# Matmuls on zeros in TensorE's opening gaps, one store for an output tile, and the last tile in reused memory

## Chip, cores and metric

One core of one Trainium2 chip. The time is the device time in microseconds (us) of one execution; lower is better. Fast executions of one kernel here spread over about 1.5% (354 to 359 us for the kernel before). PE is TensorE, DVE VectorE, ACT ScalarE, POOL GpSimd, SP SyncE, whose only work here is to issue transfers. "Clock" is the TensorE clock that was granted, as a share of full speed. A DMA transfer is moved in packets by up to 16 DMA engines; the profile shows packets and their sizes, not which engine moved them.

## The reference

Attention with RMS-normalised queries and keys (batch 8, 12 heads, 448 rows, head dimension 64), then a feed-forward stage with two multiplied branches:

```python
q_n, k_n = rmsnorm(q, g_q), rmsnorm(k, g_k)
attn = softmax(q_n @ k_n.T / sqrt(64))
x = (attn @ v) moved to (3584, 768)      # rows (b, s), columns (h, d)
h = (x @ w1) * (x @ w2) @ w3             # d_ff = 1024
out = h @ w_out                          # (3584, 768), float32
```

## The kernel before

A planner runs while the program is built: it simulates all engines with fixed durations and fixes the order of every instruction on every engine. Work for ACT, DVE, SP and POOL is added as jobs with an engine, an assumed duration, a key and what it needs; `pe_step` chooses what PE does next. `w3 @ w_out` is multiplied once, so that an output tile is one product of `abT` with `w34s`.

The columns of `abT` are ordered (j, p) within a batch, where output row = 7 p + j, p is 0 to 63 and j 0 to 6. A tile of 128 columns is thus two values of j with 64 rows each, in partitions 0 to 63 and 64 to 127. Each half is stored by its own transfer:

```python
            def store(x):
                nc.sync.dma_start(
                    out=out_rows(bp, t, x),          # [64, 768]: 64 rows, 7 rows apart
                    in_=hold["o"][HP * x : HP * x + HP].rearrange("p z n -> p (z n)"),
                )
            ...
                for x in range(2):
                    add("SP", 0.57, -20.0, lambda x=x: store(x), ...)
...
    def pe_step(t):
        took = pe_try(t, t - MARGIN)
        return pe_try(t, t) if took is None else took
...
    def do_last(t, z):                               # the last tile, in two halves
        ...
        o_sb = out_pool.tile([128, 2, NH], FP, tag="o_sb", name="o_sb")
...
        nc.vector.memset(warm_t, 0.0)
        ...
        warm(WARM)                                   # 15 matmuls of 512 columns on zeros
```

(The lines with "..." leave parts out, and the comments are added here.)

## Time and profile before

| | before |
|---|---|
| median of 3 runs | 357.58 us (355.82 to 359.0) |
| span of the profiled run | 355.0 us, clock 0.995 |
| PE busy | 97% |
| stores of the output | 54 of 192 KB, 4 of 96 KB |

The prediction below shows PE's side of this profile. What turned out to matter lies with the transfers. From the page: what was moved in how many packets; for the two large queues (q1 is SP's, q0 GpSimd's) packets, MB and the share of the 16 DMA engines' time; and the stores (count, KB each, median us from issue to landing).

```profile
DMA packets 68360, 55.11 MB, mean 155 GB/s; under 512 B 44932, under 2 KB 62244, under 8 KB 68292
...
q1 hardware_dynamic: 49824, 36.51, 43.2%
q0 software_dynamic: 18016, 16.92, 27.5%
...
out_dram<-o_sb SPq DMA_DIRECT2D x54, 192.0 KB, 3.4
```

With the three small queues the shares sum to 72.5%: packets under way for 257 of 355 us per DMA engine, on the average of the 16. (Packets can overlap: in several stretches below the share is above 1. So 257 us is an upper figure for how long an engine was occupied.) SP's queue where the first output tiles leave (start, duration, line, what, count):

```profile
86.73 2.80 SPq L953 DMA_DIRECT2D out_dram<-o_sb  x4
90.17 3.32 SPq L516 DMA_TRANSPOSE qkT<-qks  x2
93.58 0.54 SPq L344 DMA_DIRECT2D qk_sb<-in_q_dram  x1
```

Four stores are followed at once by two transposes of queries and keys, 1.7 us each, on which the next scores depend, and by the next loads. All stand in one queue.

### The profile page before, as it was taken

The numbers are of one execution on the slowest core, as the hardware profiler recorded it, in microseconds if no ns is written. First come the engines' busy times: TensorE is split into PE (matmuls) and PEld (weight loads), VectorE is DVE, ScalarE is ACT, GpSimd is POOL, SyncE is SP. The second block draws the span as 40 slices with busy tenths as digits, with TensorE's granted clock in tenths as the row PEclk, the third lists the DMA queues.
The fourth block names the chain that finished last, engine by engine and source line by source line (L and its number), as shares of the span: only waits on it lengthen the run. The fifth ranks groups of instructions, "written<-read, shape, count | busy, mean of one in ns | idle before, by whom it ended". The sixth has DMA issues, their size and how long they took to land.

```text
span 355.0 us, 16130 instructions
## 1 busy us (share of the span) xinstructions
PE 344.0 (97%) x7352; PEld 224.0 (63%) x7352; DVE 213.2 (60%) x300; ACT 256.0 (72%) x368; POOL 75.3 (21%) x132
## 2 busy tenths in 40 slices
PE   6899999999999999999999999999999999999994
PEld 2577666656665667656657675677665656666673
DVE  4459476997998689898659757686633321222100
ACT  4579958988979999898889898766886942222122
POOL 7266633105200504013013050320320000000000
PEclk9899999999999999999999999999999999999999
DMA  8999999579997899995988959942690014000064
GB/s 191 243 262 166 254 297 253 129 159 194 237 210 201 160 173 248 228 264 56 215 241 114 244 82 259 227 52 42 119 176 2 4 46 110 29 4 2 4 179 136
DMA packets 68360, 55.11 MB, mean 155 GB/s; under 512 B 44932, under 2 KB 62244, under 8 KB 68292
## 3 DMA queue, kind: packets, MB, share of 16 engines
q1 hardware_dynamic: 49824, 36.51, 43.2%
q0 software_dynamic: 18016, 16.92, 27.5%
q8 instruction: 57, 0.93, 1.1%
q10 hardware_dynamic: 452, 0.66, 0.6%
q14 instruction: 11, 0.09, 0.1%
HBM read 46.66 MB, written 11.01 MB: 162 GB/s over the span
## 4 chain that ended last, share of the span: by engine, by line
PE 84%; DMA 6%; ACT 5%; DVE 1%; POOL 1%; issue 1%; SPq 0%; DVEq 0%; POOLq 0%; ACTq 0%
PE ps_all L817 61%; PE ps_all L716 11%; PE ps_all L631 9%; DMA qk_sb<-in_q_dram 5%; PE ps_all L695 2%; ACT w_outs L653 1%; ACT P L653 1%; ACT sq L419 1%; PE ps_all L1064 1%; DMA out_dram<-o_sb 1%; ACT a_sb L329 1%; POOL w3s L397 0%; DVE qks L449 0%; PE ps_all L1086 0%; POOL w_outs L403 0%
## 5 line engine op out<-in xcount | busy, mean ns | idle before, releaser
L653 ACT ACTIVATE P<-ps_all 128x896 bf16<-128x896 f32 x120 | 104.5, 923 | 17.6 <-PE ps_all L631 17.3
L368 POOL DMA_DIRECT2D v_sb<-in_v_dram x96 | 57.2, 616 | 173.6 <-PE ps_all L631 75.4
L817 PE MATMUL ps_all<-xT,w1s 64*64 64x448 bf16 x1536 | 88.7, 349 | 0.0
L817 PE MATMUL ps_all<-xT,w2s 64*64 64x448 bf16 x1536 | 88.6, 349 | 0.0
L817 PE MATMUL ps_all<-w34s,abT 64*64 64x384 bf16 x1728 | 80.7, 323 | 0.0
L897 DVE TENSOR_TENSOR abT<-ps_all,a_sb 128x896 bf16<-128x896 f32 x32 | 34.9, 1089 | 50.8 <-PE ps_all L817 50.6
L817 PEld LDWEIGHTS <-abT 64*64 64x64 bf16 x1728 | 52.2, 107 | 19.5 <-issue 0.6
L631 PE MATMUL ps_all<-qkT 64*64 64x448 bf16 x672 | 62.0, 357 | 1.6 <-ACT w_outs L653 0.8
L817 PEld LDWEIGHTS <-w1s 64*64 64x64 bf16 x1536 | 48.7, 107 | 23.4 <-issue 0.4
L817 PEld LDWEIGHTS <-w2s 64*64 64x64 bf16 x1536 | 48.1, 107 | 24.1 <-issue 0.5
L426 DVE TENSOR_REDUCE ssq<-sq 128x14 f32<-128x896 f32 (+1 forms) x50 | 51.3, 1041 | 13.7 <-ACT sq L419 13.3
L449 DVE TENSOR_TENSOR qks<-qk_sb,al 128x448 bf16<-128x448 f32 x96 | 55.7, 617 | 1.8 <-ACT al L438 1.7
L419 ACT ACTIVATE sq<-qk_sb 128x896 f32<-128x896 f32 (+1 forms) x50 | 45.1, 916 | 4.0 <-DMA qk_sb<-in_q_dram 3.6
L329 ACT ACTIVATE a_sb<-ps_all 128x896 bf16<-128x896 f32 x22 | 20.2, 919 | 29.7 <-PE ps_all L817 29.7
L758 DVE TENSOR_TENSOR xT<-ps_all,r 128x448 bf16<-128x448 f32 x48 | 27.4, 616 | 13.1 <-ACT r L739 10.8
L335 DVE COPY o_sb<-ps_all 128x768 f32<-128x768 f32 (+1 forms) x16 | 14.1, 881 | 32.9 <-PE ps_all L1006 15.8
L631 PEld LDWEIGHTS <-qkT 64*64 64x64 bf16 x672 | 22.7, 107 | 15.3 <-issue 6.1
L329 ACT ACTIVATE o_sb<-ps_all 128x768 f32<-128x768 f32 (+1 forms) x15 | 11.2, 746 | 23.7 <-PE ps_all L817 22.0
L716 PE MATMUL ps_all<-P,v_sb 128*32 128x448 bf16 x480 | 26.7, 352 | 0.0
L817 PE MATMUL ps_all<-w_outs,w3T 64*64 64x384 bf16 x512 | 25.0, 324 | 0.5 <-DVE w3T L335 0.4
L716 PEld LDWEIGHTS <-v_sb 128*32 128x32 bf16 x608 | 16.6, 97 | 12.0
L653 ACT ACTIVATE w_outs<-ps_all 128x896 bf16<-128x896 f32 x24 | 21.2, 915 | 3.5 <-PE ps_all L631 3.2
(60 smaller groups left out, 225.5 us busy)
## 6 DMA issues: line engine op xcount, KB each, us to landing
out_dram<-o_sb SPq DMA_DIRECT2D x54, 192.0 KB, 3.4
qk_sb<-in_q_dram SPq DMA_DIRECT2D x18, 448.0 KB, 4.3
qk_sb<-in_k_dram SPq DMA_DIRECT2D x18, 448.0 KB, 5.2
v_sb<-in_v_dram POOLq DMA_DIRECT2D x48, 64.0 KB, 3.9
v_sb<-in_v_dram POOLq DMA_DIRECT2D x48, 48.0 KB, 4.1
qk_sb<-in_q_dram POOLq DMA_DIRECT2D x5, 448.0 KB, 10.5
qk_sb<-in_k_dram POOLq DMA_DIRECT2D x5, 448.0 KB, 10.9
w3s<-in_moe_w_dram POOLq DMA_DIRECT2D x8, 256.0 KB, 8.2
```

The costliest lines, as they stand in the source:

```text
L329: nc.scalar.activation(out=out, in_=in_, func=AF.Copy, scale=1.0 if by is None else by)
L335: nc.vector.tensor_copy(out=out, in_=in_)
L368: nc.gpsimd.dma_start(out=v_bufs[i % 4][p0 : p0 + HP, g::2, 0 : j1 - j0].rearrange("p h j d -> p h (j d)"), in_=src[:, g::2, j0:j1].rearra ...
L419: nc.scalar.activation(out=s["sq", t][:, x0:x1], in_=src[:, t, x0:x1], func=AF.Square)
L426: nc.vector.tensor_reduce(out=s["ssq"][:, t, x0:x1], in_=s["sq", t][:, x0:x1], axis=AX, op=ADD)
L449: nc.vector.tensor_tensor(out=s["qks"][:, t, :, x], in0=src[:, t, x], in1=s["alpha"][:, t, x].unsqueeze(2).broadcast_to([NP, NJ, D]), op=MULT,
L631: nc.tensor.matmul(out=sc[HP * c : HP * c + HP, u, 0:S].rearrange("p (j s) -> p j s", j=NJ), lhsT=qkT[u * D : (u + 1) * D, 1, j, cols], rh ...
L653: lambda: nc.scalar.activation(out=dst, in_=sc[:, :, 0:S], func=AF.Exp),
L716: nc.tensor.matmul(out=ps_all[hd * HALF : (hd + 1) * HALF, z, 0:S], lhsT=value_weights(i, hd, j, kind), rhs=s["P"][:, hd, j, :] if j < NF ...
L758: lambda: nc.vector.tensor_tensor(out=xT[b][:, 2 * m + kind - 1, :], in0=ps, in1=s["r"], op=MULT),
L817: mm = nc.tensor.matmul(out=ps_all[64 * h : 64 * h + 64, p.bank + z, 0 : p.n], lhsT=lhsT[64 * r : 64 * r + 64, 64 * h : 64 * h + 64], rhs= ...
L897: nc.vector.tensor_tensor(out=abT[bp][:, f0 : f0 + 2, odd * S : (odd + 1) * S], in0=ps_all[:, z : z + 2, 0:S], in1=a_sb[b, f0], op=MULT,)
```

## The change

Three parts: keep PE's clock up while it waits for the first data; store 18 of the 28 output tiles by one instruction in place of two; spare the last copies a wait for a buffer.

```diff
@@ ffn2_pair: one store for a tile that lies in one batch
+            flat = lambda: hold["o"].rearrange("p z n -> p (z n)")
+            whole = bp < B // 2 - 1 and 2 * t // NJ == (2 * t + 1) // NJ
...
+            def store_whole():
+                bb, j = divmod(2 * t, NJ)
+                r0 = (2 * bp + bb) * S
+                rows = out[r0 : r0 + S].rearrange("(p j) n -> j p n", j=NJ)
+                nc.sync.dma_start(out=rows[j : j + 2], in_=flat())
...
+                if whole:
+                    add("SP", 0.6, -20.0, store_whole, ..., moves=(1.1, 0.14))
+                    return
@@ do_last
-        o_sb = out_pool.tile([128, 2, NH], FP, tag="o_sb", name="o_sb")
+        spare = qk_bufs[0].rearrange("p w x j d -> p (w x j d)")
+        o_sb = spare[:, x * NH : (x + 1) * NH].rearrange("p (z n) -> p z n", z=1)
@@ pe_step (WARM_TO = 13.0, WARM_N = 256)
-        return pe_try(t, t) if took is None else took
+        took = pe_try(t, t) if took is None else took
+        if took is None and t < WARM_TO and idle_banks(t):
+            return do_warm(single(idle_banks(t)))       # one matmul on zeros
+        return took
```

The output side of `store_whole` has the shape [2, 64, 768]: two values of j outermost, then 64 rows, then 768 columns.

More of the change, by code (lines that the diff above doesn't have):

```diff
@@ L243 @@
     WARM = 15
+    WARM_TO = 13.0
+    WARM_N = 256
     MAX_PAIRS = 2
@@ L950, in copy @@
                 copy_on(engine, hold["o"], ps_all[:, z : z + 2, 0:NH])
+            flat = lambda: hold["o"].rearrange("p z n -> p (z n)")
+            whole = bp < B // 2 - 1 and 2 * t // NJ == (2 * t + 1) // NJ
             def store(x):
                 nc.sync.dma_start(
-                    out=out_rows(bp, t, x),
-                    in_=hold["o"][HP * x : HP * x + HP].rearrange("p z n -> p (z n)"),
-                )
+                    out=out_rows(bp, t, x), in_=flat()[HP * x : HP * x + HP]
+                )
+            def store_whole():
[3 more added lines that the diff above has]
+                nc.sync.dma_start(out=rows[j : j + 2], in_=flat())
             def copied(e):
                 freed(z)(e)
+                if whole:
+                    add(
+                        "SP", 0.6, -20.0, store_whole,
+                        needs=[lambda: e + SEM], moves=(1.1, 0.14),
+                    )
+                    return
                 for x in range(2):
@@ L1126, in pe_step, with do_warm @@
         took = pe_try(t, t - MARGIN)
-        return pe_try(t, t) if took is None else took
+        took = pe_try(t, t) if took is None else took
+        if took is None and t < WARM_TO and idle_banks(t):
+            return do_warm(single(idle_banks(t)))
+        return took
+    def do_warm(z):
+        nc.tensor.matmul(
+            out=ps_all[:, z, 0:WARM_N], lhsT=warm_t[:, 0:128], rhs=warm_t[:, 0:WARM_N],
+            start=True, stop=True,
+        )
+        into("t")
+        return pass_us(WARM_N)
     def start_pv(t, size, idle):
```

## The prediction

> **What bounds the kernel now.** I read the page first, then PE's waits, then the clock and busy time stretch by stretch, then the instructions of the opening and of the end in order of time. The page's busy shares and slices:
>
> ```profile
> PE 344.0 (97%) x7352; PEld 224.0 (63%) x7352; DVE 213.2 (60%) x300; ACT 256.0 (72%) x368; POOL 75.3 (21%) x132
> ...
> PE   6899999999999999999999999999999999999994
> ...
> PEclk9899999999999999999999999999999999999999
> ```
>
> PE is busy almost everywhere and no other engine is near it, so PE is the bound. The one slice in which the clock falls below 9 tenths is the second, from 8.9 to 17.8 us. PE's waits:
>
> ```profile
> PE ps_all L1064 <- DVE qks L449: 2.3, 2, 1.8
> PE ps_all L1244 <- DVE warm_t L1227: 1.2, 1, 1.2
> PE ps_all L631 <- ACT w_outs L653: 0.8, 2, 0.4
> PE ps_all L631 <- DVE qkT L335: 0.7, 1, 0.7
> ```
>
> All named waits of PE sum to about 7 us, most of it before 12 us. A check that busy is also fed: four 64x64 quarters run together, and the chain shows ten such groups of 448 columns in 1.89 us, 0.189 us a group. The FFN's first stage has 3072 matmuls, 768 groups, 145 us; the 384-column products 2240 matmuls, 560 groups at 0.163, 91 us; scores 168 groups, 32; probabilities times values 228 groups, 43; half-row sums about 7; transposes and the last tile about 10. That is 328 us of the 341.5 between the first transpose (8.8 us) and the last matmul (350.3). Only some 13 us are slack, scattered. Now the opening, by stretches. Columns: stretch, its length, then busy time with counts of PE, PEld, DVE, ACT, POOL, then the clock, the DMA share and GB/s:
>
> ```profile
> 7.00:10.50 3.50, 1.14 (x15) 0.79 (x14) 3.43 (x9) 0.52 (x2) 0.58 (x1) 1.00 1.15 207
> 10.50:11.20 0.70, 0.02 (x4) 0.02 (x4) 0.62 (x1) 0.00 (x0) 0.41 (x1) 0.81 1.07 199
> 11.20:12.00 0.80, 0.80 (x8) 0.17 (x8) 0.00 (x0) 0.18 (x1) 0.19 (x1) 0.50 1.13 213
> 12.00:13.00 1.00, 1.00 (x12) 0.77 (x8) 0.00 (x0) 1.00 (x2) 0.59 (x1) 0.50 1.14 209
> 13.00:14.00 1.00, 1.00 (x10) 0.26 (x10) 0.69 (x1) 0.86 (x2) 0.59 (x1) 0.50 1.14 206
> 14.00:14.70 0.70, 0.70 (x12) 0.59 (x16) 0.00 (x0) 0.70 (x2) 0.17 (x1) 0.76 1.16 211
> ```
>
> PE does 1.16 us of work between 7.0 and 11.2, and then its clock stands at half from about 11.0 to 14.4: a stretch of about 3.4 us, exactly when the first scores and the first w3 transposes come. The same work cold and, later, warm:
>
> ```profile
> 11.18 0.96 PE L631 MATMUL ps_all<-qkT 64*64 64x448 bf16 x8 [0.72 <-DVE qkT L335]
> 12.07 1.03 PE L1086 MATMUL ps_all<-ident,w3s 128*128 128x128 bf16 x8
> 13.04 0.96 PE L631 MATMUL ps_all<-qkT 64*64 64x448 bf16 x8
> 13.93 0.80 PE L1086 MATMUL ps_all<-ident,w3s 128*128 128x128 bf16 x8
> ...
> 15.44 0.62 PE L1086 MATMUL ps_all<-ident,w3s 128*128 128x128 bf16 x8
> ...
> 36.40 0.57 PE L631 MATMUL ps_all<-qkT 64*64 64x448 bf16 x8
> ```
>
> The end, in order of time:
>
> ```profile
> 347.48 2.83 PE L1006 MATMUL ps_all<-w34s,abT 128*64 128x192 bf16 x64
> ...
> 350.54 0.33 ACT L329 ACTIVATE o_sb<-ps_all 128x192 f32<-128x192 f32 x1 [1.13 <-DMA out_dram<-o_sb]
> 350.71 0.36 DVE L335 COPY o_sb<-ps_all 128x192 f32<-128x192 f32 x1 [1.35 <-DMA out_dram<-o_sb]
> ```
>
> The last two copies wait for an earlier store out of the same buffer, but PE had only just finished, at 350.31.
>
> **What the skill says.** The Trainium skill, "TensorE: Matmul & The Clock Gate", Part 1 (HAM clock gate), states that PE runs at 1.2 GHz after an idle window of about 3.4 us and at 2.4 GHz after a busy one, the window running free of the kernel. The trace agrees: 0.50 for about 3.4 us, after 4.2 nearly empty microseconds. The same page, "Back-to-back issue gap", gives N/2.4 ns + 2.5 warm; 448 columns make 0.189 us, which is what the chain measures, so one filling matmul of 256 columns is estimated at 0.109 us. "DMA: Bandwidth & Descriptors", "Anatomy of one DMA", puts some 2 us of fixed time, mostly completion, on each transfer; here a 96 KB store at the end landed in 2.7 us. "Perfetto Trace Analysis" warns in its opening note that matmul busy time is a bad measure since matmuls are pipelined; hence my count by groups, which gives 328 us where the page says 344.
>
> **The change part by part.**
>
> *Filling.* The build's planner emits one 256-column matmul on zeros wherever PE would have nothing to do before its time 13.0. Idle places from 7.0 to 13: about 1.8 us before the first transpose, 0.5 before the second, 0.7 before the first scores, a few tenths after: near 4 us, so some 35 matmuls of 0.109 us. They lie in time that PE does not use; a mistimed one delays real work by about a tenth. What they buy is the cold stretch: scores 2 x (0.96 - 0.57) = 0.78 us, transposes (1.03 - 0.62) + (0.80 - 0.62) = 0.59, the first w34 products 0.84 against about 0.67 = 0.17: 1.5 us of PE time. Not all of it can be taken. POOL's waits show the first three pieces of w3 landing at about 12.0, 13.3 and 14.5. With a warm clock the second transposes could begin at 13.35 rather than 13.93, four groups of products would follow until 14.6, the third transposes would end at 15.1 rather than 15.99: **about 0.85 us** gained at that point. From 15.4 to 24.2 PE works without a gap, its 144 matmuls from 18.2 at 0.168 us a group, so the gain passes through; after that PE is full until 110 us. I take 0.7 us at the end, the rest lost to data that lands no sooner (the DMA share is near full up to 53 us).
>
> *One store per tile.* 28 tiles, less the last, make 54 stores of 192 KB; six tiles of seven in the first three pairs of batches lie in one batch, so 36 stores become 18 of 384 KB. The bytes and rows are the same. It removes 18 issues of 0.57 us from SP, 10 us of a queue that nothing waits for long, and 18 completions that no copy waits for: apart from the last two, no o_sb copy is shown waiting for a store. The last pair of batches keeps its split stores. **0 us**, give or take the order that the planner makes of it.
>
> *The last tile.* Its copies go to memory that was the first queries', long dead. The first half waited for PE alone and took 0.1 us to start (matmuls half done at 348.9, copy at 349.00). The second half could start at 350.42 instead of 350.54 and 350.71; the later one counts, as both stores wait for both halves: **0.3 us**.
>
> Sum: 0.7 + 0 + 0.3 = 1.0 us. From the median of 357.58 that is 356.6. The three runs before spread over 3.2 us; if part of that is where the cold window falls, filling removes bad cases, and I put the expected time a little lower, at **356.2**.
>
> **The rivals.** (1) *The gain dies in the opening.* q, k and w3 arrive as before; PE waits in a new place for w3, the second half of w_out (landing about 18.3) or the first weights at 51 us. For it: the DMA share above 1 from 3.5 to 29 us. Against: w3's fourth and fifth pieces have landed by about 24.6 but are used at 26.96, and after 29 us PE shows no wait for a DMA. Time then 357.2. (2) *Fillers get in the way.* If the planner thinks a result comes later than it does, or if zeros run at half clock for the first microseconds, real work queues behind them. The first transposes came at 8.83; 13 fillers cold would end at about 9.8. Against: the clock was 1.00 from 7.0 to 10.5. Time then up to 358.5. (3) *The new order matters more than the parts.* The planner fixes the order of all engines at the build, and small shifts early, or fewer stores, change who goes first between 60 and 150 us, where ACT is also 85 to 99% busy and PE loses 0.85 us between 110 and 120. Nothing in the profile tells the sign; I allow 2 us either way. (4) *Every microsecond counts in full*: 1.5 and a little from the stores give 355.3.
>
> **Range and chances.** A 2% change is 7.15 us. All that the profile offers to these three parts is 1.8 us; only a lucky or unlucky order could add more, and the slack of PE altogether is 13 us. So within 2% is nearly certain: 0.95, faster 0.03, slower 0.02. The range is the 1 us gain with 2 us for order and about 1 us for run to run, combined: 353.8 to 358.4.
>
> **What would show it.** The clock should read 1.00 in all stretches from 7 to 18 us, eight scores take 0.57 us and eight transposes 0.62, and the products after the third transposes begin 0.6 to 1.0 us earlier. Some 30 to 40 new matmuls of about 0.11 us spacing should stand between 7 and 13. The stores should number 36 + 4, and no stretch after 60 us change by more than its order explains. The last two copies should start within 0.15 us of PE's end. The prediction is wrong if the order after 60 us moves PE's gaps by more than 2 us, if PE stays cold despite fillers, or if fillers delay the first transposes beyond 9.1.

## The result, and the profile after

| | before | after |
|---|---|---|
| median | 357.32 us (4 runs) | 439.31 us (437.34 to 440.02, 4 runs) |
| ratio of fast runs | | 1.228 (1.2215 to 1.2353) |
| profiled span, clock | 355.0 us, 0.995 | 437.1 us, 0.932 |

A ratio is the mean time of one kernel's fast runs over that of the other's fast runs of the same rounds, so not quite the ratio of the medians. The change costs 23%; within 2% had been given 0.95.

Of the page after, the lines that answer to those above and to those in the prediction:

```profile
PE 367.9 (84%) x7380; PEld 240.9 (55%) x7380; DVE 213.2 (49%) x299; ACT 258.2 (59%) x369; POOL 75.4 (17%) x132
...
PE   8999999990699967799778797724998689999996
...
PEclk9999999996879978989989999876999699999999
DMA  9999995995986999996979979954239910111036
...
DMA packets 67819, 55.10 MB, mean 126 GB/s; under 512 B 44392, under 2 KB 61704, under 8 KB 67752
...
q1 hardware_dynamic: 49284, 36.51, 55.7%
...
out_dram<-o_sb SPq DMA_DIRECT2D x18, 384.0 KB
out_dram<-o_sb SPq DMA_DIRECT2D x18, 192.0 KB
```

PE has 28 matmuls more (7380 against 7352), the fillers. Its first slice is up from 6 to 8 tenths, and the first nine slices show no loss. From the tenth slice, about 98 us, PE has holes, and in them the clock falls. PE is also busy 23.9 us longer (367.9 against 344.0 us), of which the fillers are about 3. SP's queue moved the same 36.51 MB, but its packets took 55.7% of 437 us in place of 43.2% of 355. The page counts 541 fewer packets, 540 of them from the class under 512 bytes.

The stretch from 90 to 130 us, before and then after (columns as in the prediction):

```profile
90.00:130.00 40.00, 39.15 (x864) 25.07 (x860) 32.36 (x46) 37.34 (x54) 7.13 (x12) 1.00 0.94 198
```

```profile
90.00:130.00 40.00, 24.55 (x456) 14.43 (x452) 17.84 (x24) 18.67 (x26) 2.38 (x4) 0.79 1.08 138
```

The compute engines do between a third and two thirds of the work that they did before. The DMA engines count as no less busy (1.08 against 0.94) but move 138 GB/s in place of 198. What PE waits for is in SP's queue and in PE's instructions after the first new stores:

```profile
85.24 2.20 SPq L966 DMA_DIRECT2D out_dram<-o_sb  x2
88.68 16.00 SPq L518 DMA_TRANSPOSE qkT<-qks  x2
104.78 0.61 SPq L346 DMA_DIRECT2D qk_sb<-in_q_dram  x1
...
108.86 0.59 PE L633 MATMUL ps_all<-qkT 64*64 64x448 bf16 x4 [10.50 <-DMA qkT<-qks]
```

The two transposes that took 3.32 us take 16.00, the next loads are issued at 104.8 in place of 93.6 us, and PE stands 10.5 us for the transposed queries and keys. PE's holes go on to about 380 us; the last whole-tile store is issued at 382.7, and the stores of the last batches are still in halves.

The trace's DMA records tell how the store travels. Its 3072-byte packets (one row each) were counted by how many were under way at the same time:

```
us with n store packets under way      n = 1    2    3   4-12  13 and more
before                                    9.5  2.0  1.7   14.9   28.2
after                                    11.1  135.2 6.2   3.6   11.9
```

After, 135 us pass with exactly two packets under way, at a median 0.121 us for 3072 bytes, 25 GB/s each; before, half of the time 13 or more. That is what a store moved by **two DMA engines** looks like. The page's packet count says the same: if each engine that takes part writes one small completion packet, 36 stores over 16 engines wrote 576, and 18 over two write 36. The difference is 540, the number found.

The reason can be looked up. The Trainium skill, "DMA: Bandwidth & Descriptors", section "Why a DMA increments its semaphore by 16 and not by 1", paragraph on the number of engines: the largest number up to 16 is taken that divides the size of the slowest dimension on both sides. For [64, 768] that is 16; for [2, 64, 768] it is 2. The trace agrees, with its 540 packets and 135 us.

### The profile page after: what moved, and what is told of

The parts are those of the page before. It is cut to its first block, busy times and chain, and to the rows that moved or that the text cites. A ratio compares the mean times of both kernels' runs of the same rounds, so it can differ in the third digit from the quotient of the medians.

```text
span 437.1 us, 16154 instructions
## 1 busy us (share of the span) xinstructions
PE 367.9 (84%) x7380; PEld 240.9 (55%) x7380; DVE 213.2 (49%) x299; ACT 258.2 (59%) x369; POOL 75.4 (17%) x132
## 2 busy tenths in 40 slices
DMA packets 67819, 55.10 MB, mean 126 GB/s; under 512 B 44392, under 2 KB 61704, under 8 KB 67752
## 3 DMA queue, kind: packets, MB, share of 16 engines
q1 hardware_dynamic: 49284, 36.51, 55.7%
q0 software_dynamic: 18016, 16.92, 23.9%
## 4 chain that ended last, share of the span: by engine, by line
PE 64%; DMA 13%; ACT 10%; issue 5%; SPq 4%; DVE 3%; DVEq 0%; ACTq 0%
PE ps_all L819 46%; PE ps_all L718 7%; PE ps_all L633 6%; DMA qk_sb<-in_q_dram 6%; DMA qk_sb<-in_k_dram 5%; ACT P L655 4%; SPq L518 3%; ACT sq L421 2%; DMA qkT<-qks 2%; PE ps_all L1273 1%; ACT w_outs L655 1%; PE ps_all L697 1%; DVE qks L451 1%; ACT r L740 1%; PE ps_all L1081 1%
## 5 line engine op out<-in xcount | busy, mean ns | idle before, releaser
L819 PE MATMUL ps_all<-xT,w2s 64*64 64x448 bf16 x1536 | 97.8, 368 | 16.1 <-issue 13.1
L819 PE MATMUL ps_all<-xT,w1s 64*64 64x448 bf16 x1536 | 97.6, 366 | 6.8 <-issue 6.8
L633 PE MATMUL ps_all<-qkT 64*64 64x448 bf16 x672 | 68.4, 367 | 29.4 <-DMA qkT<-qks 14.8
L819 PEld LDWEIGHTS <-w2s 64*64 64x64 bf16 x1536 | 54.0, 112 | 42.1 <-issue 19.4
L819 PEld LDWEIGHTS <-w1s 64*64 64x64 bf16 x1536 | 55.0, 112 | 31.2 <-issue 10.0
L819 PEld LDWEIGHTS <-abT 64*64 64x64 bf16 x1728 | 56.1, 107 | 19.1 <-issue 3.7
L451 DVE TENSOR_TENSOR qks<-qk_sb,al 128x448 bf16<-128x448 f32 x96 | 55.7, 617 | 3.8 <-ACT al L440 3.7
L633 PEld LDWEIGHTS <-qkT 64*64 64x64 bf16 x672 | 27.4, 109 | 46.5 <-issue 22.5
L718 PE MATMUL ps_all<-P,v_sb 128*32 128x448 bf16 x480 | 29.9, 373 | 9.2 <-issue 9.2
L655 ACT ACTIVATE Pr<-ps_all 128x896 bf16<-128x896 f32 x24 | 22.3, 929 | 3.4 <-PE ps_all L633 3.4
L331 ACT ACTIVATE o_sb<-ps_all 128x768 f32<-128x768 f32 x13 | 10.5, 810 | 22.0 <-PE ps_all L819 22.0
```

The source lines that it names most:

```text
L331: nc.scalar.activation(out=out, in_=in_, func=AF.Copy, scale=1.0 if by is None else by)
L451: nc.vector.tensor_tensor(out=s["qks"][:, t, :, x], in0=src[:, t, x], in1=s["alpha"][:, t, x].unsqueeze(2).broadcast_to([NP, NJ, D]), op=MULT,
L633: nc.tensor.matmul(out=sc[HP * c : HP * c + HP, u, 0:S].rearrange("p (j s) -> p j s", j=NJ), lhsT=qkT[u * D : (u + 1) * D, 1, j, cols], rh ...
L655: lambda: nc.scalar.activation(out=dst, in_=sc[:, :, 0:S], func=AF.Exp),
L718: nc.tensor.matmul(out=ps_all[hd * HALF : (hd + 1) * HALF, z, 0:S], lhsT=value_weights(i, hd, j, kind), rhs=s["P"][:, hd, j, :] if j < NF ...
L819: mm = nc.tensor.matmul(out=ps_all[64 * h : 64 * h + 64, p.bank + z, 0 : p.n], lhsT=lhsT[64 * r : 64 * r + 64, 64 * h : 64 * h + 64], rhs= ...
```

## The experiments

Theory A: the two engines are the whole loss. Rivals: B, the planner's new order of all engines; C, a new wait on the reused memory; D, a single large transfer with one completion; E, the number or size of transfers. All results were correct. "Before" was run beside each group.

### One part at a time

The kernel before with each part alone, and the change without its store.

**Filling alone**

> The kernel before with the filling matmuls alone. Theory A (the single store of a whole tile, moved by two of the 16 DMA engines, is the whole loss): 355.5 to 356.5 us, about 1.4 us faster than before, clock 1.00 from 7 to 18 us, first output copy near 84.3 us as in the changed kernel. Rival B (the filling reshuffles the order of all engines so badly that loads and transposes come late): over 400 us.

**Whole-tile store alone**

> The kernel before with only the store of a whole tile by one transfer. Theory A: 435 to 445 us, with stretches of 70 to 100 GB/s and transposes that take 8 to 16 us to issue after each such store; 540 small packets fewer than before (36 x 16 completion writes become 18 x 2). Rival B: within 1% of 357.

**Last tile alone**

> The kernel before with only the last tile's copies put into the first queries' memory. Theory A: 0.2 to 0.3 us faster, so 357.0 and not separable from before by time; in the trace the last two copies start within 0.15 us of PE's end. Rival C (the reused memory brings a new wait): slower, with a wait on a load or a scaling of the first queries before the last copies.

**Filling and last tile**

> The changed kernel without the whole-tile store: both other parts. Theory A: 355 to 356.5 us, which is what the prediction said for all three parts. Rival B: over 400 us.

| | median, runs | ratio to before |
|---|---|---|
| before | 356.61 (39) | |
| filling | 357.58 (12) | 1.0003 (0.9978 to 1.0028) |
| whole-tile store | 434.01 (4) | 1.215 (1.206 to 1.224) |
| last tile | 355.81 (12) | 0.9993 (0.9964 to 1.0022) |
| filling and last tile | 356.76 (20) | 1.0016 (0.9995 to 1.0037) |

The store alone makes 77 of the 82 us; the other 5 come only with the other parts added and are not explained. Neither of the other parts loses time without it, so rivals B (for the filling) and C fall. The median of 434 is a little under the expected 435, and its page has the expected 44392 small packets. (Its profile is of a slow run; nothing else is read from it.) Filling does not gain the expected 1.4 us: that was a miss, taken up below. Of the last tile, the trace shows what time cannot. Second half of the last tile, with the change of memory alone:

```profile
346.12 2.83 PE L1006 MATMUL ps_all<-w34s,abT 128*64 128x192 bf16 x64
...
348.98 0.36 DVE L335 COPY qk_sb<-ps_all 128x192 f32<-128x192 f32 x1 [0.96 <-PE ps_all L1006]
348.99 0.33 ACT L329 ACTIVATE qk_sb<-ps_all 128x192 f32<-128x192 f32 x1 [0.99 <-PE ps_all L1006]
```

The copies start 0.03 and 0.04 us after PE's end at 348.95; before it was 0.23 and 0.40. The estimated 0.3 us is there (0.40 to 0.04 for the later copy, one profile each), below what 12 runs resolve.

### The same order, the same bytes, other engines

```diff
@@ f1: the changed kernel, every order kept, two transfers for a tile
-                nc.sync.dma_start(out=rows[j : j + 2], in_=flat())
+                for x in range(2):
+                    nc.sync.dma_start(
+                        out=rows[j + x], in_=flat()[HP * x : HP * x + HP])
@@ f2: one transfer, outermost dimension 64
+                nc.sync.dma_start(
+                    out=rows[j : j + 2].rearrange("x p n -> p x n"), in_=flat())
@@ f2: for that, the products are written with the two j interleaved by column
+   out=abT[...].rearrange("k (t p x) -> k t x p", x=2), in0 and in1 as "k (t x p) -> k t x p"
@@ f3 (n = 62), f4 (n = 48), d1 (n = 49), d2 (n = 57): the kernel before, each half store cut
+                for p0, p1 in ((0, n), (n, HP)):
+                    nc.sync.dma_start(out=out_rows(bp, t, x)[p0:p1], in_=...[p0:p1])
```

> The changed kernel with its own order of every engine (the planner still sees one store of 0.6 us per whole tile), but each of the 18 whole-tile stores written as two transfers of 64 rows. Theory A (two engines of 16): 355 to 357 us. Rival B (the order that the planner made of fewer stores): stays at 435 to 440 us.

> The changed kernel, 18 stores of 384 KB by one transfer each, but with the two rows of a pair in neighbouring partitions, so that the output side's outermost dimension is 64 and not 2. VectorE writes the products in that order, in three instructions instead of one, which the planner does not know. Theory A: 355 to 360 us (the extra instructions may cost 1 to 3 us). Rival D (a single transfer of 384 KB with one completion is what blocks the queue, however many engines move it): 430 us or more. Small packets: 540 minus 18 x 14 = 288 fewer than before if 16 engines take part.

> The kernel before, no other part of the change, with every 64-row store cut into 62 and 2 rows, each of which 16 does not divide: two engines each. Same order of engines, less per transfer than before. Theory A: 190 KB over two engines at about 25 GB/s each is 3.7 us, half as long as a whole tile but twice as many, so a loss of the same kind, 390 to 450 us. Rivals B and D: within 2% of the control with 48 and 16 rows.

> The control for the run with 62 and 2 rows: the same number of transfers and bytes, cut into 48 and 16 rows, both multiples of 16. Theory A: 357 to 360 us, no more than the additional 54 issues cost. Rival E (more or smaller transfers are what hurts): as slow as 62 and 2.

| | stores | engines each | median, runs | ratio |
|---|---|---|---|---|
| before | 54 of 192 KB | 16 | 356.62 (54) | |
| changed | 18 of 384 KB, 18 of 192 KB | 2 and 16 | 439.31 | 1.228 |
| f1 | 54 of 192 KB | 16 | 357.61 (20) | 1.0034 (1.0010 to 1.0058) |
| f2 | 18 of 384 KB, 18 of 192 KB | 16 | 358.78 (20) | 1.0064 (1.0042 to 1.0086) |
| f3 | 54 of 186 KB, 54 of 6 KB | 2 and 2 | 497.57 (4) | 1.394 (1.386 to 1.401) |
| f4 | 54 of 144 KB, 54 of 48 KB | 16 and 16 | 359.93 (19) | 1.0087 (1.0054 to 1.0121) |

The engines of each row follow from the rule and are confirmed by the small packets. The page lines of f2, f3 and f4 in that order:

```profile
DMA packets 68072, 55.11 MB, mean 155 GB/s; under 512 B 44644, under 2 KB 61956, under 8 KB 68004
```

```profile
DMA packets 67712, 55.11 MB, mean 111 GB/s; under 512 B 44284, under 2 KB 61596, under 8 KB 67644
```

```profile
DMA packets 69224, 55.11 MB, mean 152 GB/s; under 512 B 45796, under 2 KB 63108, under 8 KB 69156
```

Against the 44932 of before: f2 has 288 fewer (18 stores fewer, 16 packets each); f3 648 fewer (54 x 4 in place of 54 x 16); f4 864 more (54 x 32 in place of 54 x 16). All fit exactly. (f4's page is of a slow run; only counts are read from it.)

f1 has, instruction for instruction, the changed kernel's order on PE, DVE, ACT and POOL, and comes back to 357.6: rival B falls entirely. Its SP queue at the place of the 16 us:

```profile
85.30 4.31 SPq L967 DMA_DIRECT2D out_dram<-o_sb  x4
89.71 2.63 SPq L518 DMA_TRANSPOSE qkT<-qks  x2
92.43 0.55 SPq L346 DMA_DIRECT2D qk_sb<-in_q_dram  x1
```

f2 has the single 384 KB transfers and loses nothing but 0.6%: rival D falls. (Part of that 0.6% may be the extra VectorE instructions, three where there was one; this was not separated.) f3 and f4 carry no part of the change and issue equally many transfers; only the place of the cut differs, and it makes 138 us: rival E falls. f3's loss was larger than the expected range of 390 to 450. That expectation reckoned with twice as many slow stores as in the change; 54 against 18 is three times as many.

### How the loss grows, and whether another queue helps

> The kernel before with its 64-row stores cut into 49 and 15 rows: 7 and 15 engines if the number is the largest up to 16 that divides the rows. 54 x 150 KB over 7 engines at 25.4 GB/s is 0.85 us each, a quarter of the 3.75 us of 62 rows over two. Theory A with a dose: 360 to 372 us, between the 360 of 48 and 16 rows and the 498 of 62 and 2. A rival in which any number that 16 does not divide is handled slowly: near 498. Small packets: 54 x 22 - 864 = 324 more than before.

> The kernel before with its 64-row stores cut into 57 and 7 rows: 3 and 7 engines. Estimate by load per engine: the page of before has 72% of the span on each engine, 257 us; 54 x 57 packets of 0.121 us on three engines are 124 us each in place of an even share of 26, so 355 us of work on the busiest three. The same sum gives 377 for the changed kernel, which took 60 us more than that, and 437 for 62 and 2 rows, which also took 60 more. Theory of the overfull engine: 385 to 425 us, about 415. Rival (the loss grows with the bytes times the time of one store alone): 54 x 2.3 us x 0.65 = 80, so 437. Small packets: 54 x 10 - 864 = 324 fewer than before.

> The changed kernel with its whole-tile stores, still 2 x 64 rows and so still two engines, issued by ScalarE's queue instead of SyncE's, where all q and k loads and the transposes are issued. Theory F (loads and transposes stand behind the store in the same queue on those two engines): most of the loss goes, under 375 us, and no transpose takes 8 us to issue. Rival G (two engines are simply overfull, whichever queue feeds them): 420 us or more.

> The changed kernel with its whole-tile stores, 2 x 64 rows, issued by GpSimd. If GpSimd's transfers choose engines by the same rule, two of 16: 420 us or more. If they use all 16: 357 to 362 us, and the store's packets run about 12 at a time as in before.

| | engines | estimated work of the busiest engine | median, runs |
|---|---|---|---|
| before | 16 | 257 us | 357 |
| d1, rows 49 and 15 | 7 and 15 | about 281 us | 363.5 (2, one of them slow; fast 360.5) |
| d2, rows 57 and 7 | 3 and 7 | 359 us | 427.6 (2) |
| changed | 2 and 16 | 377 us | 439.3 (4) |
| f3, rows 62 and 2 | 2 and 2 | 437 us | 497.6 (4) |
| h1, changed, store from ACT's queue | 2 | | 431.0 (2) |
| h2, changed, store from GpSimd's queue | 2 to 4 by its packets | | 434.0 (4, one slow) |

By the small packets the rule holds for d1 and d2 too: 45256 and 44608 are 324 more and 324 fewer than before, as expected.

The estimate: 257 us for every engine from the page of before, less an even share of the store's packets at their median of before, 0.134 us, plus those packets at 0.121 us each on the engines that carry them (the smaller pieces on the same ones; the 355 in d2's expectation leaves them out). For the changed kernel: 18 x 128 packets are 279 us, 139 on each of two engines, in place of 19, so 257 + 139 - 19 = 377. While the sum stays well below the kernel's time the loss is small (d1); where it reaches the time, it is large. Where the loss is large, the measured times lie 61 to 69 us above the estimate; that this is the opening without stores and the waits in between is argued, not shown. d2 came out at 427.6, above the expected 385 to 425 and between the 415 that this sum gave beforehand and the 437 of its rival: it does not decide between the two. That the loss grows as the engines become fewer is shown.

Another queue does not help. From ACT's queue (h1) the time is 431 and two transposes at 102 us still take 13.75 us, so it is not a matter of standing behind the store in SP's queue alone:

```profile
102.06 13.75 SPq L518 DMA_TRANSPOSE qkT<-qks  x2
```

From GpSimd's (h2) the small completion packets are 16 per store (4451 of them in all, where the changed kernel has 4199 and before 4739), but the data still went in the main two, and at times four, packets at once (68 and 26 us), at 434 us. The access pattern is at fault, not the issuer.

h2 also speaks against reading the estimate as the cause. A store that travels alone there has two packets under way, and with four each packet still takes the same 0.234 us for its 6144 bytes; so two stores were then moved at once, most likely by different engines, and the work does not all lie on the same two. Yet the loss is nearly as large. That a store occupies its two engines for about 8 us (64 packets of 0.121 us each), and that transfers which need a share of them wait that long, would fit h2 as well as the other runs; neither this nor that one engine's total runs over is shown.

### What the filling does

The window in which the first scores run, in filling alone, and in the kernel with the last tile alone, which has no fillers but happened to keep its clock:

```profile
11.20:14.70 3.50, 3.50 (x57) 2.10 (x56) 1.38 (x2) 3.05 (x4) 1.76 (x3) 1.00 1.14 208
```

```profile
11.20:14.70 3.50, 3.50 (x60) 2.07 (x56) 1.38 (x2) 3.27 (x4) 1.75 (x3) 1.00 1.13 208
```

Both have 1.00 where the first profile of before had 0.50 to 0.76. So the cold stretch need not be there without fillers. The fast runs of before, sorted by the clock of the whole run, on the three chips of the first 12 runs: clock 0.999 or more, mean 355.6 us (25 runs); 0.993 to 0.996, like the first profile (0.995, with one stretch of 3.4 us at half clock), 356.2 us (28 runs); under 0.990, mean 358.1 us (38 runs). One cold stretch thus goes with 0.6 us. The runs under 0.990 take 2.5 us more and must have been at half clock for over 7 us (1% of 355 us, twice). Where, is not shown, since no such run of before was profiled; f4's profile (0.991, a slow run without fillers) has 0.50 from 10.3 to 17.1 us. But the filled kernels with 0.999 or more take 357.0 us (filling alone, 8 runs; filling and last tile, 12 runs), 1.4 us more than before takes when it is warm. Three runs look for the reason.

```diff
@@ g1: fillers by hand, unknown to the planner, in a fixed bank: 13, 7 and 8
+            fill(13)                      # after the opening's last warm(1)
+        if i == 0:
+            fill(8 if w else 7)           # after the two first transposes
@@ g2: g1 and the last tile's memory         @@ g3: only the 8
```

> The kernel before with the same 28 filling matmuls (13, 7 and 8) written in at the three places by hand, so that the planner does not know of them and every other instruction keeps the order of before. In the runs so far before takes about 355.5 us where its clock was full and 358 where it fell, while the planned filling takes 357.1 with a full clock. Theory P (the few instructions that the planner moved cost what the filling gains): full clock in every run and 355 to 356 us, about 1 us faster than before. Rival Q (the fillers themselves, or loads that come no sooner, cost it): 356.8 to 357.5 us.

> The same with the last tile's copies in the first queries' memory: the two harmless parts in the order of before, the version that should be best if Theory P holds. Theory P: 354.7 to 355.8 us. Rival Q: about 357.

> The order of before with only the 8 filling matmuls ahead of the first scores. If 8 keep the clock full in nearly every run and it is the fillers' number that costs the filled kernels 1.4 us against before's full-clock runs: 355.5 to 356. If loads that land no sooner take the lead back whatever fills the gap: 356.8 to 357.3 with a full clock. If 8 do not keep it warm: as before, 356.7 with clocks spread from 0.988 to 1.

| | median, runs | ratio | clocks |
|---|---|---|---|
| g1 | 356.99 (22) | 1.0013 (0.9994 to 1.0032) | 0.993 to 1.000 |
| g2 | 357.22 (22) | 1.0010 (0.9986 to 1.0034) | 0.993 to 1.000 |
| g3 | 355.88 (6) | 0.9969 (0.9930 to 1.0008) | 0.994 to 1.000 |

g1 keeps the order of every instruction of before (its trace agrees) and shows the same as the planned filling: theory P falls, it is not the few moved instructions. Where the lead goes is seen from the start of the softmax sums (the first matmuls on P and ones of a pair of head groups) in one profile each, in us:

| | at 3rd mark | 7th | 11th | 12th | 14th |
|---|---|---|---|---|---|
| before (cold) | 46.05 | 128.66 | 220.72 | 247.57 | 286.39 |
| last tile alone (warm by chance) | 44.67 | 126.88 | 219.12 | 246.21 | 285.03 |
| filling alone | 45.03 | 127.18 | 220.13 | 247.99 | 286.80 |
| g1 | 45.21 | 127.42 | 218.95 | 248.13 | 286.94 |
| g3 | 44.70 | 126.92 | 218.41 | 245.47 | 284.28 |

All warm openings lead by 0.8 to 1.4 us at 45 us and by 1.2 to 1.8 at 127. g1 gives its lead back between the 11th and the 12th mark, at one pair of loads. Last tile alone, then g1: the issue of the load, and the squares that wait for it:

```profile
213.36 1.59 SPq L344 DMA_DIRECT2D qk_sb<-in_q_dram  x1
...
219.28 2.04 ACT L419 ACTIVATE sq<-qk_sb 128x896 f32<-128x896 f32 x2 [0.95 <-DMA qk_sb<-in_q_dram]
```

```profile
213.41 0.96 SPq L344 DMA_DIRECT2D qk_sb<-in_q_dram  x1
...
221.64 2.04 ACT L419 ACTIVATE sq<-qk_sb 128x896 f32<-128x896 f32 x2 [3.47 <-DMA qk_sb<-in_q_dram]
```

The load is issued at the same time, but its data are used 8.2 us after and not 5.9. g2 shows the same place (7.9 us); filling alone has lost most of its lead before the 11th mark, between 127 and 151 us, and some there. Why the load takes longer in the filled kernels is open: nothing in the traces ties it to 28 fillers at 7 to 11 us. With 8 fillers the lead stays, and the mean of six runs is 0.3% below before, but the interval reaches 1: a hint that fewer fillers suffice, not a finding. No version here is shown to beat before; g3 is the best candidate.

## Why the prediction was wrong

**The bound.** PE was the bound, rightly read, with a slack of some 13 us. But "no other engine is near it" was said of the compute engines, and the DMA engines, with their 72%, were not weighed. (Two slips on which nothing large rests: PE's named waits sum to 5.9 us, not about 7; and the idle places listed for the fillers sum to 3 us and some tenths, not near 4.)

**The store** is the step that failed: "The bytes and rows are the same. It removes 18 issues of 0.57 us from SP, 10 us of a queue that nothing waits for long ... **0 us**". Bytes and rows are the same, but not the access pattern, and with it the number of DMA engines fell from 16 to 2. The term put at 0 us measured +77 us alone (434.0 against 356.6), of +82 in the change (439.3 against 357.3). That "nothing waits for long" for SP's queue held of before only: with two engines carrying 139 us of store packets each in place of 19, two transposes behind the first such stores took 16.0 us in place of 3.3, and PE stood 10.5 us for them. The rule was to be had beforehand, on the page of the Trainium skill named above; it was not held against the new shape. None of the four rivals had it: where they speak of stores, they look for the effect in order and time saved.

**The filling.** The mechanism was right as far as 127 us: the clock is 1.00, the first eight scores take 0.57 us, and a lead of 1.2 us stands at the third transposes (14.26 in place of 15.44) and of 1.2 to 1.8 at 127, more than the 0.85 estimated for 16 us. One term of it did not exist: the first w34 products took 0.84 us warm as cold. The fillers were 28 where some 35 were guessed, and the first transposes, at 8.6 us, were not delayed. Of the 0.7 us at the end nothing is seen: filling alone changed the time by 0.1 us (-0.8 to +1.0), which does not exclude a gain of 0.7; filling and last tile by 0.6 (-0.2 to +1.3), which does. In the profiles the lead is given back at loads past 127 us; that is the prediction's first rival, but far later than it was placed. The guess that the spread of before is partly the cold stretch fits: runs with a full clock took 355.6, with one stretch's worth of low clock 356.2, with more 358.1 us.

**The last tile.** About 0.36 us by the trace, 0.3 as worked out, and too little to be seen in the times.

**The range.** "All that the profile offers to these three parts is 1.8 us" is a bound on gains. It was used as a bound on losses too, and that gave "slower" 0.02. Without its store the change lies where the prediction put the whole (356.76, within 353.8 to 358.4).

## What to carry to other kernels

When a transfer is merged, reshaped or reordered, look at the outermost dimension on both sides before anything else: the largest number up to 16 that divides both says how many engines move it (62 gives 2, 49 gives 7), and the count of small packets on the page before and after showed it here every time for SP's stores. If two slices must go in one transfer, put the dimension that 16 divides outermost, even at the price of another layout on chip (f2), or leave them as two transfers (f1). And a lead gained early can be lost at later loads, as here: compare the same mark late in both traces before counting it.

## What the Trainium skill lacked or had wrong

- "DMA: Bandwidth & Descriptors", section on the semaphore increment: the rule for the number of engines held in every shape tried (64, 2 x 64, 64 x 2, 62 and 2, 48 and 16, 49 and 15, 57 and 7 rows), to the packet. What it lacks is the consequence for everything else: transfers over two engines delay other transfers that use all 16, and took this kernel from 357 to 439 and, in f3, to 498 us.
- The same page, "Measured", advises to batch transfers to 1 MiB or more. The caution on shape is on the page, but far from that advice, in "Rules for kernel authors": an outermost dimension under 16 confines the transfer to at most that many engines. What the page lacks is the price: batching 192 KB to 384 KB cost 21.5% where the merged dimension of 2 came outermost, and gained nothing where it did not (f2, 358.8 us).
- The same page says that GpSimd's transfers have all 16 engines post completion, and that some direct copies get 16 engines. The completion packets agree (16 per store in h2). Which copies get 16 it leaves open; this shape did not: the data moved mainly two, at times four, packets at once, and the time was 434 us.
- "TensorE: Matmul & The Clock Gate", Part 1, puts the penalty of the ramp under 1% of a span; the runs agree (0.6 of 356 us with one cold stretch, 2.5 in the runs of the lowest clock). No page warns that fillers may gain nothing: the filled kernels at full clock took 357.0 us, the kernel before at full clock 355.6.
